# Reading the first block's keys once: tap shifts on TensorE in a fused gated long-convolution and SwiGLU kernel

## The chip, the core and the metric

The kernel runs on one core of one Trainium2 chip. A core has TensorE (matrix multiply, PE in the profile; PEld is its weight load), VectorE (DVE), ScalarE (ACT), GpSimd (POOL) and SyncE (SP), which here only issues transfers; 16 DMA engines move data between HBM and SBUF, the on-chip memory of 128 partitions. Matmul results land in PSUM. The metric is the device time of one execution in microseconds (us), lower is better.

## The reference

Two sub-layers run over a sequence of 2048 tokens with 640 channels, all tensors bf16:

```
ln(x)    = (x - mean(x)) / sqrt(var(x) + 1e-5)               # over the 640 channels
kshift   = sum over t = 0..3 of  k[s - t] * shift_k[:, t]    # a causal filter of four taps; rows before 0 are zero
kv       = kshift * v
y        = causal_conv(kv, ssm_k) + kv * ssm_D               # 2048 taps per channel (by FFT in the reference)
h        = q + ln(q) * y
out      = h + (silu(ln(h) @ w_gate) * (ln(h) @ w_up)) @ w_down       # 640 -> 1728 -> 640
```

## The kernel before, in words

**Tiling.** The sequence is cut into four blocks of 512 tokens (`n` = 0..3), a block into four tiles of 128 tokens (`q` = 0..3), one token per partition. The long convolution becomes a sum of block products in a transformed domain of 2 x 512 coefficients ("c" and "s" halves, four row tiles of 128 each). The filter's four blocks are transformed once (`g_transform(p)`: 64 matmuls against the basis `WG`, evicted by ACT, L296). Block n's `kv` is transformed by `x_transform(n)` (32 matmuls against `WX`, evicted by ACT, L364). `pair(j, p)` multiplies block j's transform with the filter's part p elementwise on DVE (eight operations of 128x2560 for a whole pair). `inverse(n)` goes back to tokens by matmuls against `WI`, adds the mirrored half by matmuls against a reversal matrix `flip`, multiplies with `ln(q)`, adds q, computes the second layer norm, and hands the result to `ffn(n)` by a transposing DMA into `hT`. `ffn(n)` makes 14 column chunks: five gate matmuls into bank 0 of a PSUM tile, five up matmuls into bank 1, silu (L530) and a copy (L531) on ACT, a product on DVE (L533), and then 112 down matmuls (L542).

**The taps.** `front(n)` makes `kv`. For each tile, `front_tile` holds four shifted copies of k side by side (`k4`, 128 x 4 x 640, read by one overlapping DMA of 640 KB a tile), multiplies them with the tap weights `w4` (L315), adds them in two steps (L316, L317) and multiplies with v (L318). In block 0, `first_loads` fetches the four shifted tiles by k loads of 560, 640 and 1280 KB and four small ones from POOL for the rows at the edge, which a POOL memset (L332) zeroes first. `w4` is spread over the partitions by `wcast`: a matmul with a row of ones and an ACT copy for each tap (L278, L280). The first two tiles of `kv` are also reversed in token order by matmuls with `flip` (L347) into `rev`, and L350 and L351 form the difference and the sum that `x_transform` takes.

**Layer norms.** `ln` takes the sums by two ACT passes (L436: mean, L437: mean square; the order between them is free), except for the second layer norm of block 0, which DVE does. POOL then runs four tiny operations (L443 to L446) to get 1/sqrt(var + eps), and DVE scales (L451).

**Order of work.** Every operation is given to a planner with an engine, an assumed duration, what it reads and writes, a priority `pr` (lower first) and sometimes an earliest time `t0`. `Plan.order` runs a list schedule over these, and the instructions are written out in that order, so each engine's queue is fixed in advance. PSUM has two tiles each of kind A (front, x_transform, inverse) and F (g_transform, ffn). Assumed durations are helpers: `act(n)` for an eviction, a lag of 0.12 us from one engine to another, 1.7 us for the POOL part of a layer norm. Transfers go through the queues of SP and ACT, and a few through POOL; the planner models eight transfers in flight, and a ninth waits for the oldest. Two instructions that touch the same PSUM tile are ordered in the order they are written, even where they touch different banks of it. In block 0 the filter's part 0 has priority -5, ahead of the front (0 to 3) and of `x_transform(0)` (8).

## Time and profile before

| | us |
|---|---|
| median of 5 runs (310.83 to 312.32) | 311.78 |
| the profiled execution's own time | 311.13 |
| its span, first to last instruction | 309.3 |
| PE busy | 269.1 (87%), 1540 matmuls recorded |
| DVE busy | 231.1 (75%), 307 instructions |
| ACT busy | 164.6 (53%) |
| POOL busy | 112.3 (36%) |
| moved by DMA | 45.94 MB |

Busy time of an engine is the union of its instructions' spans; matmuls are pipelined, so PE can be busy without running at its peak. The table of stages gives busy time by stretch of the span; the timeline lists instructions with start, duration, and in brackets the idle time of the engine before them with what released it; the chain is the sequence of work that ended last, followed back from the end. A row's line number is that of the code above.

### The profile page before, as it was taken

The page shows a single profiled execution, that of the slowest core. Times are in us where ns is not written, and L with a number is a line of the kernel's source. Part 1 is how long each engine was busy: PE and PEld are TensorE (multiplying, and loading weights), DVE is VectorE, ACT ScalarE, POOL GpSimd, SP SyncE. Part 2 cuts the span into 40 slices and gives each one's busy share as a digit, 9 for nine tenths or more (in the row PEclk, how much of TensorE's full clock was granted, in tenths as well). Part 3 has the DMA queues.
Part 4 walks back from the last instruction along what each step waited for, and adds up shares of the span by engine and source line. Part 5 has one row for each costly group of instructions (what it writes and reads, how often), then busy time and mean ns, then how long its engine had stood idle before and what let it go on. Part 6 is the DMA issues. An engine that isn't in the chain of part 4 may idle for free.

```text
span 309.3 us, 4282 instructions
## 1 busy us (share of the span) xinstructions
PE 269.1 (87%) x1540; PEld 151.1 (49%) x1556; DVE 231.1 (75%) x307; ACT 164.6 (53%) x318; POOL 112.3 (36%) x132
## 2 busy tenths in 40 slices
...
GB/s 186 316 352 188 375 184 208 2 126 329 214 85 127 99 172 215 135 291 176 87 123 68 105 210 190 103 201 85 138 147 57 24 95 32 130 143 133 0 45 42
DMA packets 71943, 45.94 MB, mean 149 GB/s; under 512 B 30772, under 2 KB 69492, under 8 KB 71794
## 3 DMA queue, kind: packets, MB, share of 16 engines
...
q8 instruction: 12, 0.20, 0.3%
q0 software_dynamic: 160, 0.08, 0.1%
q14 instruction: 9, 0.07, 0.1%
...
## 4 chain that ended last, share of the span: by engine, by line
PE 39%; DVE 32%; DMA 13%; ACT 6%; issue 5%; POOL 4%; ACTq 0%; POOLq 0%; DVEq 0%
PE psF L524 22%; DVE s L369 10%; PE psF L542 8%; DMA s<-const_wg 5%; PE psF L293 4%; DVE T L369 4%; DMA hT<-hl 4%; PE psA L361 4%; DVE k L315 3%; DMA WI<-const_wi 2%; DVE tT L533 2%; DVE y L490 2%; DVE o L547 2%; POOL sm L443 2%; ACT uc L531 1%
## 5 line engine op out<-in xcount | busy, mean ns | idle before, releaser
L443 POOL TENSOR_TENSOR sm<-sm 128x1 f32<-128x1 f32 x28 | 40.5, 1445 | 117.1 <-ACT junk L436 117.1
L524 PE MATMUL psF<-hT,wg 128*128 128x512 bf16 x268 | 69.9, 384 | 9.6 <-DMA hT<-hl 8.7
L524 PE MATMUL psF<-hT,wu 128*128 128x512 bf16 x256 | 65.3, 384 | 2.9 <-ACT sg L530 2.2
L542 PE MATMUL psF<-wd,tT 128*128 128x320 bf16 x448 | 64.9, 299 | 1.1 <-ACT uc L531 0.9
L530 ACT ACTIVATE sg<-psF 128x512 bf16<-128x512 f32 (+1 forms) x56 | 33.5, 598 | 53.6 <-PE psF L524 53.6
L542 PEld LDWEIGHTS <-tT 128*128 128x128 bf16 x448 | 41.4, 97 | 24.7 <-issue 9.6
L524 PEld LDWEIGHTS <-wg 128*128 128x128 bf16 x280 | 27.4, 99 | 41.8 <-issue 12.3
L533 DVE TENSOR_TENSOR tT<-sg,uc 128x512 bf16<-128x512 bf16 (+1 forms) x56 | 23.6, 422 | 32.4 <-ACT uc L531 32.2
L369 DVE TENSOR_TENSOR s<-s,T 128x2560 bf16<-128x2560 bf16 x32 | 47.3, 1486 | 0.0
L369 DVE TENSOR_TENSOR T<-s,s 128x2560 bf16<-128x2560 bf16 x32 | 47.3, 1486 | 0.0
L524 PEld LDWEIGHTS <-wu 128*128 128x128 bf16 x260 | 25.6, 99 | 33.2 <-issue 5.4
L293 PE MATMUL psF<-wd,s 128*128 128x320 bf16 x192 | 29.8, 314 | 9.9 <-DMA s<-const_wg 9.5
L293 PEld LDWEIGHTS <-s 128*128 128x128 bf16 x256 | 25.8, 101 | 21.8 <-DMA s<-const_wg 10.2
L531 ACT CAST uc<-psF 128x512 bf16<-128x512 f32 (+1 forms) x56 | 32.6, 582 | 5.6 <-PE psF L524 5.5
L446 POOL TENSOR_TENSOR sm<-sm,mhalf 128x1 f32<-128x1 f32 x32 | 31.6, 989 | 2.7
L296 ACT CAST s<-psF 128x640 bf16<-128x640 f32 x32 | 22.1, 694 | 17.3 <-PE psF L293 17.3
L361 PE MATMUL psA<-kv,WX 128*128 128x320 bf16 x128 | 22.1, 316 | 4.7 <-DMA WI<-const_wi 3.9
L436 ACT ACTIVATE junk<-x 128x640 bf16<-128x640 bf16 x28 | 20.7, 740 | 3.6 <-DVE x L491 3.3
L547 DVE TENSOR_TENSOR o<-psF,x 128x640 bf16<-128x640 f32 x16 | 13.1, 819 | 12.5 <-PE psF L542 12.5
L364 ACT CAST s<-psA 128x640 bf16<-128x640 f32 x32 | 21.4, 702 | 0.7 <-PE psA L361 0.5
L437 ACT ACTIVATE junk<-x 128x640 bf16<-128x640 bf16 x28 | 20.8, 743 | 0.4
L315 DVE TENSOR_TENSOR k<-k,w 128x2560 bf16<-128x2560 bf16 x14 | 20.7, 1484 | 0.3 <-DMA k<-in_A_k_dram 0.3
...
## 6 DMA issues: line engine op xcount, KB each, us to landing
...
```

Source lines behind the costliest of these rows:

```text
L293: nc.tensor.matmul(ps(g)[:, h, 0:NH], WG[:, kt, ct * P:(ct + 1) * P], gT[p][:, kt, h * NH:(h + 1) * NH], start=(kt == 0), stop=(kt == 3))
L296: add("ACT", act(D), lambda g=g, ct=ct: nc.scalar.copy(r3(G[p][ct // 4][:, ct % 4, :]), ps(g)[:, :, 0:NH]), r=[g], w=[Gk[p] + "cs"[ct // 4 ...
L315: add("DVE", dve(4 * D), lambda: nc.vector.tensor_mul(kd[:], kd[:], w4[:]), r=["w4"] + ks, w=[kn], pr=pr)
L361: nc.tensor.matmul(ps(g)[:, h, 0:NH], WX[:, kt, ct * P:(ct + 1) * P], kv[:, base + kt, h * NH:(h + 1) * NH], start=(kt == 0), stop=(kt == 1))
L369: add("DVE", dve(n * D), lambda: f(o, a, b), r=ks(ak) + ks(bk), w=ks(ok), after=["WG0", "WG1"] if ok[:2] == "s7" else [], pr=pr)
L443: e.tensor_tensor(s[:, 2:3], s[:, 0:1], s[:, 0:1], op=ALU.mult)
L446: e.tensor_tensor(s[:, 4:5], s[:, 3:4], mhalf[:], op=ALU.pow)
L524: nc.tensor.matmul(ps(gr)[:, which, :], w[:, kt, cc * P:(cc + 1) * P], hT[b][:, kt, :], start=(kt == 0), stop=(kt == 4))
L530: add("ACT", act(MB), lambda gr=gr, s=s, z=z: nc.scalar.activation(sg[s][:z, :], ps(gr)[:z, 0, :], ACT.Silu), r=[(gr, 0)], w=[f"sg{s}"], p ...
L531: add("ACT", act(MB), lambda gr=gr, s=s, z=z, merged=merged: nc.scalar.copy(uc[s][:z, :], ps(gr)[64:128, 0, :] if merged else ps(gr)[:, 1, ...
L533: add("DVE", dve(MB), lambda c=c, s=s, z=z: TM(tT[:z, c * MB:(c + 1) * MB], sg[s][:z, :], uc[s][:z, :]), r=[f"sg{s}", f"uc{s}"], w=[f"tT{c ...
L542: nc.tensor.matmul(ps(gr)[:, h, 0:NH], tT[:z, c * MB + m * P:c * MB + (m + 1) * P], wd[:z, c, h * NH:(h + 1) * NH], start=(c == 0), stop=( ...
```

## The change

k of block 0 is loaded once (640 KB, `kfirst`, into the buffer of block 1's x). `front_first` multiplies each k tile with all four taps in one DVE operation (the k tile is repeated by a broadcast operand), and the shift by 0 to 3 rows together with the sum over taps is done on PE: eight matmuls for the first tile, fourteen for each of the others (three taps also take rows from the tile before), with 128-column windows of a constant `perm` that holds an identity, its mirror image and zeros. For the first two tiles the window is mirrored, so the result comes out reversed; v of these two tiles is reversed on PE too and copied out by ACT. DVE multiplies the PSUM result with v. Three of the eight evictions of `x_transform(0)` go to DVE. `g_transform(0)` has priority 9 instead of -5, and the evictions of every `g_transform` go ahead of ACT's other work.

In the layer norm, ACT's first pass gives minus the mean and the second pass takes it as its bias, so that it sums squared deviations; POOL does two operations instead of four. In the feed-forward part, silu (bank 0) and the up matmuls (bank 1) are declared independent of each other. The planner's lag from one engine to another becomes 0.22 us from PE and 0.24 us from ACT, `act(n)` becomes shorter, and some priorities and earliest times are set anew. Nothing else of the computation changes.

```diff
...
 def make_flip():
-    f = np.eye(P)[::-1]
-    return np.ascontiguousarray(np.stack([f, -f], axis=1)).astype(ml_dtypes.bfloat16)
+    i, z = np.eye(P), np.zeros((P, P))
+    j = i[::-1]
+    return np.ascontiguousarray(np.stack([-j, z, j, z, i, z], axis=1)).astype(ml_dtypes.bfloat16)
...
             for u in users[i]:
-                lag = 0.0 if ops[u]["eng"] == e and e != "DVE" and not o["kb"] else 0.12
+                lag = LAG.get(e, 0.12) if ops[u]["eng"] != e or o["kb"] else 0.12 if e == "DVE" else 0.0
...
 RATE = 330.0
+LAG = {"PE": 0.22, "ACT": 0.24}
...
 def act(n):
-    return 0.19 + n / 1200
+    return 0.07 + n / 1220
...
     slot = [tl(f"s{i}", [P, 8, D]) for i in range(8)]
-    last, fourth = slot[7], slot[4]
+    last = slot[7]
...
     WI = tl("WI", [P, 8, 256])
-    flip = tl("flip", [P, 2, P])
+    perm = tl("perm", [P, 6, P])
+    flip = (perm[:, 2, :], perm[:, 0, :])
+    band = perm[:].rearrange("p a b -> p (a b)")[:, 3 * P:6 * P]
+    mirrored = perm[:].rearrange("p a b -> p (a b)")[:, P:4 * P]
...
     xin = [tl(f"x{i}", [P, 4, D]) for i in range(2)]
+    kfirst = xin[1]
+    products, prodk = [k4[0], k4[1], slot[4][0], slot[4][1]], ["k4_0", "k4_1", "s4c", "s4s"]
...
     hl = [tl(f"hl{i}", [P, D]) for i in range(2)]
-    drow = y[0][0:1, :]
+    drow = xln[0][0:1, :]
...
-    add("POOL", 0.1, lambda: nc.gpsimd.memset(ones[:], 1.0), w=["ones"], pr=-9)
+    add("POOL", 0.1, lambda: nc.gpsimd.memset(ones[:], 1.0), w=["ones"], pr=-99)
...
     add("ACT", 1.5, lambda: nc.scalar.activation(sg[0][0:1, 0:P], ones[:], ACT.Silu), r=["ones"], w=["sg0"], pr=-50)
-    load("POOL", drow, A_ssm_D.partition_broadcast(1), ["drow"], -75, 5)
+    load("ACT", drow, A_ssm_D.partition_broadcast(1), ["drow"], -95.5, 5)
...
             add("ACT", act(D), lambda g=g, ct=ct: nc.scalar.copy(r3(G[p][ct // 4][:, ct % 4, :]), ps(g)[:, :, 0:NH]),
-                r=[g], w=[Gk[p] + "cs"[ct // 4]], pr=pr, rel=("F", g))
+                r=[g], w=[Gk[p] + "cs"[ct // 4]], pr=pr - 900, rel=("F", g))
...
         kd, kn, vb, vn = k4[b], f"k4_{b}", vt[b], f"v{b}"
-        if n == 0:
-            vb, vn = hT[0][:].rearrange("p a b -> p (a b)")[:, q * D:(q + 1) * D], "v0all"
-            if q > 1:
-                kd, kn = slot[4][b], "s4" + "cs"[b]
-        else:
-            load("SP", kd[:], run(r0 - 3, P), [kn], pr - 40, 640)
-            load("SP", vb[:], vv[r0:r0 + P, :], [vn], pr - 40, 160)
-        ks = [kn] + [f"edge{i}" for i in range(5) if n == 0 and q == 0]
+        load("SP", kd[:], run(r0 - 3, P), [kn], pr - 40, 640)
+        load("SP", vb[:], vv[r0:r0 + P, :], [vn], pr - 40, 160)
+        ks = [kn]
...
     def first_loads():
-        kd = k4[0]
-        load("ACT", kd[16:128, :, :], run(13, 112), ["edge4"], -98, 560)
-        load("SP", k4[1][:], run(P - 3, P), ["k4_1"], -88, 640)
-        load("ACT", hT[0][:].rearrange("p a b -> p (a b)").rearrange("p (a b) -> p a b", a=4), vv[0:MB, :].rearrange("(m p) d -> p m d", p=P), ["v0all"], -97, 640)
-        load("ACT", WG, WG_h.ap(), ["WG0", "WG1"], -96, 1024)
-        load("SP", fourth[:].rearrange("p (m a) b -> p m (a b)", m=2),
-             bass.AP(tensor=kk.tensor, offset=kk.offset + (2 * P - 3) * D, ap=[[D, P], [P * D, 2], [1, 4 * D]]), ["s4c", "s4s"], -87, 1280)
-        add("POOL", 2.2, lambda: nc.gpsimd.memset(kd[0:32, :, :], 0.0), w=["k4_0"], pr=-90)
-        for t in range(3):
-            k = 3 - t
-            load("POOL", kd[t:t + 1, k:4, :], kk[0:t + 1, :].rearrange("(o a) d -> o a d", o=1), [f"edge{t}"], -80, 2, r=["k4_0"])
-        load("POOL", kd[3:16, :, :], run(0, 13), ["edge3"], -81, 65, r=["k4_0"])
+        load("SP", kfirst[:], kk[0:MB, :].rearrange("(m p) d -> p m d", p=P), ["x1_0", "x1_1", "x1_2", "x1_3"], -98, 640)
+        load("ACT", hT[0][:].rearrange("p a b -> p (a b)").rearrange("p (a b) -> p a b", a=4), vv[0:MB, :].rearrange("(m p) d -> p m d", p=P), ["v0all"], -96, 640)
+        load("ACT", WG, WG_h.ap(), ["WG0", "WG1"], -95, 1024)
+    def front_first(q, pr):
+        prod, pk = products[q][:], prodk[q]
+        add("DVE", dve(4 * D), lambda: nc.vector.tensor_mul(prod, kfirst[:, q:q + 1, :].to_broadcast([P, 4, D]), w4[:]), r=["w4", f"x1_{q}"], w=[pk], pr=pr)
+        g = ("A", "S", q)
+        m, turn = 1 - q, q < 2
+        def mm():
+            for h in range(2):
+                cols = slice(h * NH, (h + 1) * NH)
+                for i, (src, t, last_tile) in enumerate([(products[q], t, 0) for t in range(4)] + [(products[q - 1], t, 1) for t in range(3) if q]):
+                    j = 3 - t
+                    lhs = mirrored[:, P * (1 - last_tile) + j:][:, 0:P] if turn else band[:, P * (1 + last_tile) - j:][:, 0:P]
+                    nc.tensor.matmul(ps(g)[:, h, 0:NH], lhs, src[:, t, cols], start=(i == 0), stop=(i == (6 if q else 3)))
+        add("PE", (14 if q else 8) * 0.137, mm, r=["flip", pk] + ([prodk[q - 1]] if q else []), w=[g], pr=pr - 50, acq=("A", g))
+        v = hT[0][:].rearrange("p a b -> p (a b)")[:, q * D:(q + 1) * D]
+        if turn:
+            gv = ("F", "V", q)
+            def mv():
+                for h in range(2):
+                    nc.tensor.matmul(ps(gv)[:, h, 0:NH], flip[0], v[:, h * NH:(h + 1) * NH], start=True, stop=True)
+            add("PE", 2 * 0.137, mv, r=["flip", "v0all"], w=[gv], pr=pr - 60, acq=("F", gv))
+            add("ACT", act(D), lambda: nc.scalar.copy(r3(y[q][:]), ps(gv)[:, :, 0:NH]), r=[gv], w=[f"y{q}"], pr=pr - 60, rel=("F", gv))
+            add("DVE", dve(D, True), lambda: nc.vector.tensor_mul(r3(rev[:, m, :]), ps(g)[:, :, 0:NH], r3(y[q][:])), r=[g, f"y{q}"], w=["rev"], pr=pr, rel=("A", g))
+        else:
+            add("DVE", dve(D, True), lambda: nc.vector.tensor_mul(r3(kv[:, q, :]), ps(g)[:, :, 0:NH], r3(v)), r=[g, "v0all"], w=[f"kv{q}"], pr=pr, rel=("A", g))
...
         for q in (0, 1, 2, 3):
-            front_tile(n, q, pr + q)
-            if q < 2:
+            (front_tile(n, q, pr + q) if n else front_first(q, pr + q))
+            if q < 2 and n:
...
                     for h in range(2):
-                        nc.tensor.matmul(ps(g)[:, h, 0:NH], flip[:, 0, :], kv[:, q, h * NH:(h + 1) * NH], start=True, stop=True)
+                        nc.tensor.matmul(ps(g)[:, h, 0:NH], flip[0], kv[:, q, h * NH:(h + 1) * NH], start=True, stop=True)
...
             add("PE", 4 * 0.137, mm, r=["WX", f"kv{base}", f"kv{base + 1}"], w=[g], pr=pr, acq=("A", g), after=[Xk[n] + "cs"[ct // 4]])
-            add("ACT", act(D), lambda g=g, ct=ct: nc.scalar.copy(r3(X[n][ct // 4][:, ct % 4, :]), ps(g)[:, :, 0:NH]),
+            on_dve = n == 0 and ct in (1, 7, 4)
+            copy = nc.vector.tensor_copy if on_dve else nc.scalar.copy
+            add("DVE" if on_dve else "ACT", dve(D, True) if on_dve else act(D), lambda g=g, ct=ct, copy=copy: copy(r3(X[n][ct // 4][:, ct % 4, :]), ps(g)[:, :, 0:NH]),
...
-    def ln(n, q, which, pr, vec=False):
+    def ln(n, q, which, pr, vec=False, t0=0.0):
...
         else:
-            add("ACT", act(D) + 0.2, lambda: nc.scalar.activation(junk[:], src, ACT.Copy, scale=1.0 / D, accum_out=s[:, 0:1]), r=[xk], w=[k + "a"], pr=pr)
-            add("ACT", act(D) + 0.2, lambda: nc.scalar.activation(junk[:], src, ACT.Square, scale=float(D ** -0.5), accum_out=s[:, 1:2]), r=[xk], w=[k + "b"], pr=pr)
+            add("ACT", act(D) + 0.25, lambda: nc.scalar.activation(junk[:], src, ACT.Copy, scale=-1.0 / D, accum_out=s[:, 0:1]), r=[xk], w=[k + "a"], pr=pr, t0=t0)
+            add("ACT", act(D) + 0.45, lambda: nc.scalar.activation(junk[:], src, ACT.Square, bias=s[:, 0:1], accum_out=s[:, 1:2]), r=[xk, k + "a"], w=[k + "b"], pr=pr)
...
         def fin():
-            if vec:
-                e.tensor_scalar(s[:, 3:4], s[:, 1:2], 1.0, EPS, op0=ALU.mult, op1=ALU.add)
-            else:
-                e.tensor_tensor(s[:, 2:3], s[:, 0:1], s[:, 0:1], op=ALU.mult)
-                e.tensor_tensor(s[:, 3:4], s[:, 1:2], s[:, 2:3], op=ALU.subtract)
-                e.tensor_scalar(s[:, 3:4], s[:, 3:4], 1.0, EPS, op0=ALU.mult, op1=ALU.add)
+            e.tensor_scalar(s[:, 3:4], s[:, 1:2], 1.0 if vec else 1.0 / D, EPS, op0=ALU.mult, op1=ALU.add)
             e.tensor_tensor(s[:, 4:5], s[:, 3:4], mhalf[:], op=ALU.pow)
-        add("POOL", 1.0 if vec else 1.7, fin, r=[k + "a", k + "b"], w=[k], pr=pr)
+        add("POOL", 1.5, fin, r=[k + "a", k + "b"], w=[k], pr=pr)
...
         s = sm[n, q, which]
-        nc.vector.tensor_scalar(dst, xin[n % 2][:, q, :], s[:, 0:1], s[:, 4:5], op0=ALU.subtract, op1=ALU.mult)
+        nc.vector.tensor_scalar(dst, xin[n % 2][:, q, :], s[:, 0:1], s[:, 4:5],
+                                op0=ALU.subtract if (n, which) == (0, 2) else ALU.add, op1=ALU.mult)
...
     def load_x(n, pr, queue="SP"):
-        load(queue, xin[n % 2][:], xq[n * MB:(n + 1) * MB, :].rearrange("(m p) d -> p m d", p=P), [f"x{n % 2}_{q}" for q in range(4)], pr, 640, t0=(10, 30, 0, 0)[n])
+        load(queue, xin[n % 2][:], xq[n * MB:(n + 1) * MB, :].rearrange("(m p) d -> p m d", p=P), [f"x{n % 2}_{q}" for q in range(4)], pr, 640, t0=(14, 30, 0, 0)[n])
         for q in range(4):
-            ln(n, q, 1, pr + 30)
+            ln(n, q, 1, pr + 30, t0=(26, 50, 0, 0)[n])
...
                             for part in range(2):
-                                nc.tensor.matmul(ps(g)[:, h, 0:NH], flip[:, part, :], (es, os_)[part][m][:, h * NH:(h + 1) * NH],
+                                nc.tensor.matmul(ps(g)[:, h, 0:NH], flip[part], (es, os_)[part][m][:, h * NH:(h + 1) * NH],
...
     wcount = [0]
+    issued = {}
+    def apart(gr, bank, inst):
+        for other in issued.get((gr, 1 - bank), []):
+            tc.declare_no_dep(inst.ins if hasattr(inst, "ins") else inst, other, reason="other bank")
+        issued.setdefault((gr, bank), []).append(inst.ins if hasattr(inst, "ins") else inst)
...
                     for kt in range(5):
-                        nc.tensor.matmul(ps(gr)[:, which, :], w[:, kt, cc * P:(cc + 1) * P], hT[b][:, kt, :], start=(kt == 0), stop=(kt == 4))
+                        i = nc.tensor.matmul(ps(gr)[:, which, :], w[:, kt, cc * P:(cc + 1) * P], hT[b][:, kt, :], start=(kt == 0), stop=(kt == 4))
+                        if which:
+                            apart(gr, 1, i)
+                def silu(gr, s, z):
+                    apart(gr, 0, nc.scalar.activation(sg[s][:z, :], ps(gr)[:z, 0, :], ACT.Silu))
...
                 z = 64 if merged else P
-                add("ACT", act(MB), lambda gr=gr, s=s, z=z: nc.scalar.activation(sg[s][:z, :], ps(gr)[:z, 0, :], ACT.Silu), r=[(gr, 0)], w=[f"sg{s}"], pr=pr - 9000)
+                add("ACT", act(MB), lambda gr=gr, s=s, z=z, silu=silu: silu(gr, s, z), r=[(gr, 0)], w=[f"sg{s}"], pr=pr - 9000)
...
-    load("ACT", flip[:], J_h.ap(), ["flip"], -26, 64, t0=6)
+    load("ACT", perm[:], J_h.ap(), ["flip"], -97, 192)
...
     load("ACT", WX[:], WX_h.ap(), ["WX"], -25, 512, t0=8)
-    g_transform(0, -5)
+    g_transform(0, 9)
...
     gload(2, -20)

```

## The prediction, made before the changed kernel was run

> **What bounds the kernel now.** I read the table of stages first. The columns are the stretch in us, its length, busy time of each engine with instruction counts, granted clock, DMA share and GB/s.
>
> ```profile
> 0.00:45.30 45.30, 24.50 (x138) 14.91 (x139) 20.66 (x29) 23.11 (x42) 13.99 (x28) 0.96 1.00 272
> 45.30:76.40 31.10, 28.52 (x206) 19.89 (x204) 30.96 (x48) 23.90 (x44) 16.85 (x24) 1.00 0.53 155
> 76.40:257.70 181.30, 168.50 (x954) 92.22 (x968) 170.24 (x214) 102.45 (x205) 81.45 (x80) 1.00 0.51 138
> 257.70:309.30 51.60, 47.58 (x244) 24.04 (x247) 9.25 (x18) 15.13 (x28) 0.00 (x0) 0.95 0.28 74
> ```
>
> DVE works 20.66 of the first 45.30 us. From the first pair product (45.32) to the last feed-forward part (257.7) it works 201.2 of 212.4, so this stretch is DVE's. The last 51.6 us are PE's (`ffn(3)`), and cannot start before DVE has finished `inverse(3)`. So the time is: idle time of DVE up to 45.3, plus DVE's work, plus a PE tail. Next the chain of waits for the start, to see what keeps DVE idle.
>
> ```profile
> 3.90 15.47 DMA s<-const_wg
> 19.42 11.05 PE psF L293 x64
> 30.77 6.28 DMA WI<-const_wi
> 37.06 3.99 PE psA L361 x16
> ```
>
> The filter basis lands at 19.4, part 0 of the filter fills PE until 30.5, and the first `x_transform` comes only at 37.0. It does not read WI; the timeline shows what really came last:
>
> ```profile
> 13.52 2.87 DVE L315 TENSOR_TENSOR k<-k,w 128x2560 bf16<-128x2560 bf16 x2
> 19.40 2.88 DVE L315 TENSOR_TENSOR s<-s,w 128x2560 bf16<-128x2560 bf16 x2
> 32.74 0.43 PE L347 MATMUL psA<-kv,flip 128*128 128x320 bf16 x2
> 33.21 0.69 ACT L349 CAST rev<-psA 128x640 bf16<-128x640 f32 x1 [0.70 <-PE psA L347]
> 33.94 0.83 DVE L350 TENSOR_TENSOR kv<-kv,rev 128x1280 bf16<-128x1280 bf16 x1 [8.58 <-ACT rev L349]
> 36.08 0.82 DVE L351 TENSOR_TENSOR kv<-kv,rev 128x1280 bf16<-128x1280 bf16 x1
> 45.32 1.48 DVE L369 TENSOR_TENSOR s<-s,s 128x2560 bf16<-128x2560 bf16 x1
> ```
>
> DVE had the tile products of block 0 at 25.4; the two reversals stood in PE's queue behind the filter, DVE idled 8.58 us, and L351 (ends 36.90) released `x_transform`. Last, the waits from 45 to 257:
>
> ```profile
> DVE hl L451 <- POOL sm L446: 4.4, 5, 1.3
> DVE tT L533 <- ACT uc L531: 1.9, 4, 1.0
> PE psF L524 <- ACT sg L530: 2.2, 4, 0.9
> ```
>
> The layer norm's POOL part costs DVE 4.4 us in five waits, and PE waits 2.2 us for silu of the other bank.
>
> **Part 1, the tap weights and k.** Before, DVE starts at 13.52 because `w4` is complete at 12.84. From its first matmul (6.20, held by a POOL memset) that takes 6.6 us, of which 2.45 are ACT standing behind the WX load (issued 11.18). The memset of ones now comes first on POOL, and five loads instead of four are issued by ACT ahead of the table load (1.28): at 0.4 to 0.5 each that is 3.1 + 1.28 + 0.3 = 4.7 for the first eviction's earliest start. When the 5 KB weight row lands is not shown: by 6.2 at the latest, not before its issue ends at 1.3. I take 4, and 4 + 4.2 = 8.2 (7 to 11). k is first on SP's queue; the nearest rows are 640 KB in 8.7 us and 560 KB in 8.2, while 5.58 MB moved in the first 20 us. Now about 3.8 MB are asked for (k, v, perm, WG, two filter parts), so 7 us, landed at 7.7 (5 to 9.4). Products start at 8.2 instead of 13.5.
>
> **Part 2, DVE work of block 0.** Removed: L316 four times (3.08) and L317 four times (1.75). L318 (0.44 each, 1.75) becomes a product from PSUM at 0.82 (row L490), 3.28. Three evictions are added at the same 0.82, 2.46. The 480 ns add, four products (5.92 at 1.48) and L350/L351 (1.65) stay: 13.8 instead of 14.5, 0.7 less. The broadcast product is in no row: it is at best 1.48, at worst at the one-element rate of L490, 2560/640 x 0.74 = 2.96, which is 5.9 more in all. I take 1.48, since element step and type are those of L315.
>
> **Part 3, PE.** Added 50 shift matmuls and 4 for v, removed 4 reversals. A warm 320-column matmul comes every 0.137 us (eight in 1.09, between evictions at 25.06 and 26.15). After idle they take twice that: the first two filter groups were evicted at 21.77 and 23.90, 2.1 apart. So 16 x 0.27 + 38 x 0.137 = 9.5 us, beginning when the first product ends, 8.2 + 1.5 = 9.7: it would end at 19.2, about when DVE, at 9.2 us for four products and four PSUM products, reaches the fourth tile. One or two filter groups (1.1 each) put between them delay the last tile; with L350/L351 I take 23 for `kv` (21 to 26), 14 us before 36.9. WG has perm and v ahead on ACT's queue (832 KB, before: 1200 KB and more beside it); I take 15 (12 to 19.4). Filter 8.8 and `x_transform` 4.4 bring PE's total from 9.7 to 22.7, plus 1 to 2 of idling: 34. The first pair product needs only the "c" halves, so DVE starts it at 33 (30 to 37), against 45.32.
>
> ACT's evictions (eight and five at 0.69, two for v) make 10.4 us between 10 and 34, beside PE. The three on DVE fall where it has only block 1 to do.
>
> **Part 4, what DVE had done by then.** Before, it had also done 6.2 us of block 1 (20.66 - 14.46). Those loads go out on SP from 29.88, after the filter transposes. SP's queue loses 1280 KB; at some 160 KB/us (half of 320 GB/s, two queues) that is 8 us: issued from 22, landed from 27 (4.8 median). kfirst and the first transpose still precede gT1, and perm is 128 KB more on ACT. Between 27 and 33, less the evictions, DVE does 4.5 (2 to 6.2). Gain on DVE: 45.32 - 33 - (6.2 - 4.5) = **10.6** (6 to 15).
>
> **Part 5, the first feed-forward part on PE.** Its start at 76.44 waited for `hT`, landed 76.35. PE must by then have done 54 + 32 + 256 + 32 + 8 matmuls and two reversals, 384 x 0.137 = 52.6, 2.2 for the cold ones, from 9.7, with some 3 idle: 67.5, while DVE offers 65.8. PE gains 8.9, DVE 10.6. PE has slack later (168.5 busy of 181.3, and these ends are modelled), so I take 9.6 of the two.
>
> **Part 6, silu.** Its 2.2 us of PE waits go. Silu also starts one bank earlier (0.5 us of the 0.60 and 0.58 pair leaves the path to L533). PE does not bind there, so I count 0.8 (0 to 2.2).
>
> **Part 7, layer norm.** 56 POOL operations go; L443 (1445 ns) ran beside ACT's second pass, only L444 (525 ns) behind it. The second pass now has to wait for the first's accumulator and reads a bias. No row has either; ACT's own order bounds the wait below at 0, and the 0.17 to 0.47 that ACT stood idle before filter evictions (L296), which wait on PE, bound it above: at 0.3, 28 x 0.3 = 8.4 us of ACT at 53% busy. On DVE's waits (4.4 in five) it may gain 2 or lose 5 x 0.3 = 1.5; I take 0. The Trainium skill, "ScalarE: Activation LUTs", section "What ACT_TABLE_LOAD costs", speaks against this part: an operand of one value per partition adds about 93 ns to an ACTIVATE; by that an estimate of 2.6 us for 28 passes, and no run here shows it. The same skill, "VectorE: DVE Perf Modes", section "The DRAIN you can't avoid", says that an accumulator read by the engine's next instruction is read stale without a semaphore; the trace has no such pair.
>
> **Part 8, the planner.** For an eviction of 512 columns its duration and lag were 0.617 + 0.12 and are 0.49 + 0.24: the sum is the same. Order changes everywhere; in this stretch DVE's idle time is 11.2 us of 212, so up to 4 either way, taken as 0.
>
> **Sum.** The profiled execution took 311.13, 0.65 under the median; 311.13 - 9.6 - 0.8 = 300.7, and against the median 301.4.
>
> **Rivals.** (a) Partial gain: the pair starts earlier, but the front is dearer or FFN 0 waits for PE. For it: the broadcast bound (5.9 us more on DVE), cold matmuls, PE at 28.5 of 31.1 us before FFN 0. Against it: the step is the same as L315's. With 4 to 6 us less gain: 305 to 307. Chance 0.20. (b) Slower: the new order puts L533 ahead of its copy on ACT while DVE is the bound. There are 42 such products before 257.7; they waited 1.9 us in all. If each waits 0.3 the loss is 12.6 and the time 314; it decides from 0.25 each (10.4/42). For it: every operation is reordered, and ACT's second pass becomes longer than its assumed 0.45 more. Against it: copies come earlier with silu, and duration plus lag add up as before. Chance 0.11. (c) More gain: pair at 30, all of block 1's 6.2 us done, both silu and POOL waits gone: 311.8 - 15 - 4 = 293. Chance 0.08. (d) No effect, because FFN 0 is held by its weights or by hT: the trace has weights issued from 32.2, well ahead. Chance 0.03.
>
> **Numbers.** Likeliest 301.4, chance 0.58, own range 297 to 305. With (a) and part of (c) the range is 295 to 309. A change of 0.3% (0.9 us) is about what a measurement can tell: faster 0.86, same 0.03, slower 0.11.
>
> **What would show it.** Right: first product near 8 us, at 1.48; L351's successor ends near 23; first pair product near 33; FFN 0's first matmul at 66 to 68, FFN 3's near 248, and the tail still 51.6. No PE wait for silu. Wrong: a broadcast product over 2 us; the last shift group behind several filter groups; DVE waits on L533 summing to over 5 us before FFN 3; FFN 0 waiting for PE.

## The result and the profile after

| us | before | after | predicted |
|---|---|---|---|
| median (85 and 43 runs) | 311.17 | 312.84 | 301.4 |
| the profiled execution's own time | 311.13 | 312.32 | |
| its span | 309.3 | 310.5 | |
| first pair product on DVE | 45.32 | 41.60 | 33 |
| first matmul of FFN 0 on PE | 76.44 | 78.01 | 66 to 68 |
| first matmul of FFN 3 on PE | 257.70 | 259.92 | 248 |
| from there to the end of the span | 51.60 | 50.58 | 51.6 |

The ratio to before is 0.999, with a 95% interval of 0.9971 to 1.0009: no difference. The changed kernel's single times scatter from 307 to 319 us, those of before from 308.6 to 316.3; the ratio leaves disturbed executions out and the medians do not, which is why these two differ.

The stages of the changed kernel's profile, with the columns of the prediction's first lines, cut at its own first pair product and at FFN 3:

```profile
0.00:41.60 41.60, 25.93 (x150) 16.03 (x151) 16.77 (x17) 13.37 (x22) 0.42 (x6) 1.00 1.11 241
41.60:259.92 218.32, 202.67 (x1198) 116.64 (x1210) 203.61 (x268) 136.15 (x267) 114.73 (x64) 0.98 0.52 139
259.92:310.50 50.58, 46.62 (x244) 23.87 (x247) 9.24 (x18) 16.56 (x28) 0.00 (x0) 0.97 0.28 75
```

The pair starts 3.7 us earlier. From it to FFN 3 the time grew from 212.4 to 218.3: DVE has 203.6 us of work there instead of 201.2, because less of block 1 was done by then, and idles 14.7 instead of 11.2. So FFN 3 starts 2.2 us later, and the end gains 1.0. The start decides the rest. Its DMA issues and PE and DVE work in the timeline of after:

```profile
1.23 23.23 SPq L276 DMA_TRANSPOSE wd<-in_A_ssm_k_dram  x3
7.44 2.89 DVE L335 TENSOR_TENSOR k<-x,w 128x2560 bf16<-128x2560 bf16 x2 [7.44 <-ACT w L288]
16.56 1.22 PE L353 MATMUL psF<-hT,perm 128*128 128x320 bf16 x4 [5.29 <-DMA hT<-in_A_v_dram]
19.48 0.48 DVE L292 TENSOR_TENSOR wd<-wd,xln 1x640 bf16<-1x640 bf16 x1 [9.15 <-DMA wd<-in_A_ssm_k_dram]
28.10 0.82 DVE L373 TENSOR_TENSOR kv<-kv,rev 128x1280 bf16<-128x1280 bf16 x1
37.33 1.49 DVE L318 TENSOR_TENSOR k<-k,w 128x2560 bf16<-128x2560 bf16 x1 [3.35 <-DMA k<-in_A_k_dram]
39.61 0.70 PE L383 MATMUL psA<-kv,WX 128*128 128x320 bf16 x4 [2.94 <-DVE s L388]
41.60 1.49 DVE L393 TENSOR_TENSOR s<-s,s 128x2560 bf16<-128x2560 bf16 x1
```

The tap products begin at 7.44 and take 1.45 each, with the broadcast operand. Then two things are late at once. v, issued at 1.67, lands at 16.56 and PE idles 5.29 for it. And DVE's queue has the one-row addition of `ssm_D` (L292) ahead of the third product; it waits until 19.48 for part 0 of the filter, DVE idles 9.15, and the last two products and all that follows them stand behind it. (The two waits overlap: from 16.56 on v was there.) `kv` is complete at 28.9. The groups of issues (KB, us to landing):

```profile
s<-const_wg ACTq DMA_DIRECT2D x1, 1024.0 KB, 16.7
hT<-in_A_v_dram ACTq DMA_DIRECT2D x1, 640.0 KB, 14.9
wd<-in_A_ssm_k_dram SPq DMA_TRANSPOSE x3, 18.4
```

Three transposing loads of the filter now go out on SP right behind k. The table of stretches of 6 us shows what the 16 DMA engines did at that time (the last two columns; the share adds up the packets' times and can pass 1):

```profile
6.00:12.00 6.00, 2.96 (x11) 1.30 (x10) 2.89 (x2) 1.29 (x2) 0.00 (x0) 1.00 1.12 277
12.00:18.00 6.00, 1.44 (x6) 0.84 (x6) 0.00 (x0) 0.71 (x2) 0.00 (x0) 1.00 1.50 75
18.00:24.00 6.00, 5.21 (x28) 3.09 (x26) 4.52 (x5) 0.57 (x1) 0.00 (x0) 1.00 1.12 203
```

Between 12 and 18 the engines are busy throughout and move 75 GB/s. Before, the 1.9 MB of k loads stood between the first and the second filter transpose in SP's queue, and these stretches moved 307, 336 and 320 GB/s; the middle one was:

```profile
12.00:18.00 6.00, 0.00 (x0) 0.00 (x0) 4.89 (x6) 0.83 (x2) 0.00 (x0) 1.00 1.07 336
```

The second half of the loss stands at FFN 0, rows of SP's queue and of PE in after:

```profile
71.34 2.99 SPq L515 DMA_TRANSPOSE hT<-hl  x1
69.80 6.85 PE L301 MATMUL psF<-hT,s 128*128 128x320 bf16 x48 [0.17 <-ACT s L304]
78.01 1.24 PE L551 MATMUL psF<-hT,wg 128*128 128x512 bf16 x4 [1.36 <-DMA hT<-hl]
```

PE transforms filter parts until 76.6. Before, it had 32 matmuls of part 1 done by the first pair product; here it had none, and 8 of part 0 were left: 40 x 0.137 = 5.5 us, about as much as the stretch from the pair to FFN 0 grew (36.4 instead of 31.1). That this work is the cause is argued from the count. PE's last wait at FFN 0 is another: 1.36 us for `hT`. DVE had written its last `hl` at 69.7 (before: 71.4), but the transposing load of it was issued at 71.34, behind another one and a load of `w_down`. Before, PE waited 1.49 us for `hT` at the same place.

The waits after the start, up to FFN 3 (us, times, longest): PE's wait for silu is gone, DVE's waits for POOL sum to 4.4 as before, and PE's for `hT` to 6.7 against 8.7, both with the one at FFN 3. New is one wait of DVE for an eviction:

```profile
DVE y L499 <- ACT os L492: 4.1, 1, 4.1
DVE xln L470 <- POOL sm L465: 3.0, 2, 2.5
DVE hl L470 <- POOL sm L465: 1.4, 2, 0.7
PE psF L551 <- DMA hT<-hl: 6.7, 2, 5.3
```

### The profile page after: what moved, and what is told of

Same layout as the page of the kernel before. It is cut to its first block, busy times and chain, and to the rows that moved or that the text cites. A ratio compares the mean times of both kernels' runs of the same rounds, so it can differ in the third digit from the quotient of the medians.

```text
span 310.5 us, 4308 instructions
## 1 busy us (share of the span) xinstructions
PE 275.2 (89%) x1591; PEld 156.5 (50%) x1606; DVE 229.6 (74%) x302; ACT 166.1 (53%) x315; POOL 115.2 (37%) x70
## 3 DMA queue, kind: packets, MB, share of 16 engines
HBM read 35.97 MB, written 2.62 MB: 124 GB/s over the span
## 5 line engine op out<-in xcount | busy, mean ns | idle before, releaser
L464 POOL TENSOR_SCALAR sm<-sm 128x1 f32<-128x1 f32 x32 | 57.3, 1792 | 137.2 <-ACT junk L461 130.0
L465 POOL TENSOR_TENSOR sm<-sm,mhalf 128x1 f32<-128x1 f32 x32 | 57.4, 1793 | 2.7
L565 DVE TENSOR_TENSOR tT<-sg,uc 128x512 bf16<-128x512 bf16 (+1 forms) x56 | 23.6, 422 | 30.2 <-ACT uc L563 30.2
L563 ACT CAST uc<-psF 128x512 bf16<-128x512 f32 (+1 forms) x56 | 32.8, 585 | 16.6 <-PE psF L551 16.1
L301 PEld LDWEIGHTS <-s 128*128 128x128 bf16 x256 | 25.0, 98 | 11.1 <-issue 1.1
L301 PE MATMUL psF<-wd,s 128*128 128x320 bf16 x192 | 27.9, 299 | 0.3 <-ACT s L304 0.3
L488 PE MATMUL psA<-s,WI 128*128 128x320 bf16 x128 | 20.1, 314 | 4.3 <-DVE s L393 4.3
L460 ACT ACTIVATE junk<-x 128x640 bf16<-128x640 bf16 x28 | 20.8, 742 | 5.5 <-DVE x L511 4.7
L461 ACT ACTIVATE junk<-x,sm 128x640 bf16<-128x640 bf16 x28 | 23.4, 836 | 0.2
L383 PE MATMUL psA<-kv,WX 128*128 128x320 bf16 x128 | 20.2, 299 | 3.5 <-DVE s L388 2.9
L388 ACT CAST s<-psA 128x640 bf16<-128x640 f32 x29 | 19.0, 710 | 3.7 <-PE psA L383 3.7
## 6 DMA issues: line engine op xcount, KB each, us to landing
s<-const_wg ACTq DMA_DIRECT2D x1, 1024.0 KB, 16.7
```

Source lines behind the costliest of these rows:

```text
L301: nc.tensor.matmul(ps(g)[:, h, 0:NH], WG[:, kt, ct * P:(ct + 1) * P], gT[p][:, kt, h * NH:(h + 1) * NH], start=(kt == 0), stop=(kt == 3))
L460: add("ACT", act(D) + 0.25, lambda: nc.scalar.activation(junk[:], src, ACT.Copy, scale=-1.0 / D, accum_out=s[:, 0:1]), r=[xk], w=[k + "a"] ...
L461: add("ACT", act(D) + 0.45, lambda: nc.scalar.activation(junk[:], src, ACT.Square, bias=s[:, 0:1], accum_out=s[:, 1:2]), r=[xk, k + "a"], ...
L464: e.tensor_scalar(s[:, 3:4], s[:, 1:2], 1.0 if vec else 1.0 / D, EPS, op0=ALU.mult, op1=ALU.add)
L465: e.tensor_tensor(s[:, 4:5], s[:, 3:4], mhalf[:], op=ALU.pow)
L488: nc.tensor.matmul(ps(g)[:, h, 0:NH], WI[:, 4 * part + ct, m * P:(m + 1) * P], a[part][:, ct, h * NH:(h + 1) * NH], start=(ct == 0), stop= ...
```

## The experiments

### One part of the change alone

The first has the start alone: the changed kernel with layer norm, silu and planner as before.

```diff
-            add("ACT", act(D) + 0.25, lambda: nc.scalar.activation(junk[:], src, ACT.Copy, scale=-1.0 / D, accum_out=s[:, 0:1]), r=[xk], w=[k + "a"], pr=pr, t0=t0)
-            add("ACT", act(D) + 0.45, lambda: nc.scalar.activation(junk[:], src, ACT.Square, bias=s[:, 0:1], accum_out=s[:, 1:2]), r=[xk, k + "a"], w=[k + "b"], pr=pr)
+            add("ACT", act(D) + 0.2, lambda: nc.scalar.activation(junk[:], src, ACT.Copy, scale=1.0 / D, accum_out=s[:, 0:1]), r=[xk], w=[k + "a"], pr=pr, t0=t0)
+            add("ACT", act(D) + 0.2, lambda: nc.scalar.activation(junk[:], src, ACT.Square, scale=float(D ** -0.5), accum_out=s[:, 1:2]), r=[xk], w=[k + "b"], pr=pr)
...
-                        if which:
-                            apart(gr, 1, i)
...
-    return 0.07 + n / 1220
+    return 0.19 + n / 1200
```

> The kernel before with the first-block part alone (k read once, shifts on TensorE, three evictions on VectorE, the filter transform behind the front); layer norm, silu and the planner's constants as before. Theory A (the front itself starts the first pair only some 4 us earlier, because three filter transposes now queue together beside v and the basis, and PE is no earlier at the first feed-forward part): first pair near 41 to 42 us, first feed-forward matmul at 75 to 79, time within 1.5 us of before. Rival B (the front gains, another part gives it back): 4 to 8 us faster than before.

The second has the layer norm alone, in the kernel before.

```diff
+            add("ACT", act(D) + 0.45, lambda: nc.scalar.activation(junk[:], src, ACT.Square, bias=s[:, 0:1], accum_out=s[:, 1:2]), r=[xk, k + "a"], w=[k + "b"], pr=pr)
```

> The kernel before with the new layer norm alone (second ScalarE pass reads the first's mean, two GpSimd operations). Theory A: within 1.5 us of before either way. Rival B (GpSimd operations starved between VectorE operations give back the front's gain): 3 to 6 us slower.

The third has silu alone, in the kernel before.

```diff
+                        if which:
+                            apart(gr, 1, i)
...
+                    apart(gr, 0, nc.scalar.activation(sg[s][:z, :], ps(gr)[:z, 0, :], ACT.Silu))
```

> The kernel before with silu and the up matmuls declared independent, nothing else. Prediction's term: 0.8 us faster (0 to 2.2). Theory A and rival B both allow that. Silu should start about 1.1 us earlier than its up matmuls end, and no PE wait for silu should be left.

The fourth has the planner's constants alone, in the kernel before.

```diff
+LAG = {"PE": 0.22, "ACT": 0.24}
...
-    return 0.19 + n / 1200
+    return 0.07 + n / 1220
```

> The kernel before with the planner's new lags and eviction durations alone, so that only the order of instructions changes. Theory A: within 1.5 us of before. Rival C (the new order costs what the front gains): 3 to 6 us slower.

Measured, with the kernel before at 314.9 us in the same session (19 runs, 310.2 to 318.8): the start alone 315.23 (ratio 1.0086, 1.0007 to 1.0165), the layer norm alone 317.36 (four runs, 311.3 to 318.75, too far apart for a ratio), silu alone 320.82 (1.0252, 1.0109 to 1.0395, from three runs), the planner alone 310.92 (0.994, 0.9887 to 0.9992). The planner's term lies inside its bounds, the layer norm's can't be told, and the other two are missed: the predicted 9.6 us of the start are not there at all, though its first pair product is at 40.98, and its FFN 0 comes at 83.35, later than the 75 to 79 expected. Silu alone is slower, and neither the prediction nor the expectation had that. The profiled execution (322.99 us, the longest of the four) shows two things beside silu's own: the first pair product comes at 50.65 instead of 45.32, and DVE's waits for POOL sum to 12.1 us over the whole span, against 5.1 before:

```profile
DVE xln L451 <- POOL sm L446: 7.1, 2, 4.0
DVE hl L451 <- POOL sm L446: 5.0, 6, 1.3
```

Why its start is late was not followed up.

So two questions were open: what holds the start, and why POOL's few short operations cost more as soon as the order changes.

### The filter transposes out of the way of v and WG

First, parts 1 to 3 wait for WG, through a copy of one element by POOL into their destination.

```diff
     def gload(p, pr):
+        if p in (1, 2, 3):
+            add("POOL", 0.2, lambda: nc.gpsimd.tensor_copy(gT[p][0:1, 0, 0:1], WG[0:1, 0, 0:1]), r=["WG0"], w=[f"gT{p}"], pr=pr)
         add("SP", 2.7, lambda: nc.sync.dma_start_transpose(gT[p], A_ssm_k[:, p * MB:(p + 1) * MB]), w=[f"gT{p}"], pr=pr, kb=640)
```

> The changed kernel, with the filter transposes of parts 1 to 3 held until the basis WG has landed (a one-element GpSimd copy from WG into each destination, so that the transfer must wait for it). Theory A (the slow transposes share the DMA engines with v and WG and delay both): v lands near 7 instead of 16.5, WG near 12 instead of 19.3, the first pair starts near 33 to 36 instead of 41.6, and the time falls by 3 to 7 us. Rival D (the DMA engines are full of other work anyway): v and WG land within 2 us of where they did, time within 1.5 us.

Second, the one-row addition moves from DVE to POOL.

```diff
-    add("DVE", 0.2, lambda: nc.vector.tensor_add(gT[0][0:1, 0, :], gT[0][0:1, 0, :], drow), r=["drow"], w=["gT0"], pr=-20)
+    add("POOL", 1.0, lambda: nc.gpsimd.tensor_add(gT[0][0:1, 0, :], gT[0][0:1, 0, :], drow), r=["drow"], w=["gT0"], pr=-20)
```

> The changed kernel, with the one-row addition of ssm_D to the first filter part on GpSimd instead of VectorE, so that VectorE's products no longer stand behind it. Theory A: VectorE's third and fourth product move from 19.9 and 22.0 to near 11 to 14, but TensorE still stands behind v (16.5), so the first pair starts only 1 to 3 us earlier, time 0 to 2 us less. Rival E (the wait in VectorE's queue is what costs): first pair 6 to 9 us earlier, time 4 to 8 us less.

Third, both of these.

```diff
+        if p in (1, 2, 3):
...
+    add("POOL", 1.0, lambda: nc.gpsimd.tensor_add(gT[0][0:1, 0, :], gT[0][0:1, 0, :], drow), r=["drow"], w=["gT0"], pr=-20)
```

> Both edits: transposes held, addition on GpSimd. Theory A: first pair at 31 to 34, the start as it had been predicted; if the start sets the end, the time falls by 6 to 9 us against the changed kernel; if PE's filter transforms or later waits set it, by less than 3, and the first feed-forward matmul stays after 74.

Fourth, both, and all of block 0's `x_transform` evictions on ACT.

```diff
-            on_dve = n == 0 and ct in (1, 7, 4)
+            on_dve = False
```

> As the kernel with both edits, and the three evictions of the first transform back on ScalarE. Theory A: PE's 2.9 us of waiting for an eviction that stands on VectorE behind a k transfer goes; first pair earlier by 0 to 3 us than with both edits alone.

Measured against before at 310.86 us (309.88 to 311.92, seven runs):

| | median us | ratio (95%) | v's landing after issue | first pair product | FFN 0 |
|---|---|---|---|---|---|
| transposes 1 to 3 held | 301.82 | 0.9669 (0.9607 to 0.9731) | 10.1 | 38.12 | 74.9 |
| addition on POOL | 308.33 | 0.9888 (0.9837 to 0.9939) | 17.6 | 45.03 | 82 |
| both | 299.91 | 0.9527 (0.9445 to 0.961) | 10.7 | 31.59 | 68.56 |
| both, evictions on ACT | 299.12 | 0.9625 (0.9585 to 0.9665) | 10.0 | 33.19 | 70.0 |

Each trace column is from one profiled execution; that with the addition on POOL took 312.34, the longest of its four, and its v was the latest of these four kernels. So its pair at 45.03 says little about the addition, and its median shows a gain of 1%. With both edits the start comes near where it was predicted (pair 33, FFN 0 at 66 to 68), and the time with it. Holding is most of the effect, more than the 3 to 7 us expected; the addition's place seems to matter too, since without it the pair is at 38.12 with nearly the same landing of v. The evictions make no difference that can be told.

But holding also puts block 1's first k and v ahead of the transposes. So the next kernel keeps the changed kernel's order and its bytes, and takes away only the transposing: parts 1 to 3 are plain loads of as many bytes. (Their contents are not the filter's; this kernel leaves the transposition of these parts out.)

```diff
     def gload(p, pr):
+        if p:
+            add("SP", 2.7, lambda: nc.sync.dma_start(out=gT[p], in_=vv[p * MB:(p + 1) * MB, :].rearrange("(m p) d -> p m d", p=P)), w=[f"gT{p}"], pr=pr, kb=640)
+            return
         add("SP", 2.7, lambda: nc.sync.dma_start_transpose(gT[p], A_ssm_k[:, p * MB:(p + 1) * MB]), w=[f"gT{p}"], pr=pr, kb=640)
```

> The changed kernel in its order, with the transfers of filter parts 1 to 3 made plain ones of the same bytes (640 KB each, rows of v instead of the transposed filter; so these parts of the filter are not the reference's). Theory A (transposing transfers move some 70 GB/s while they hold the DMA engines, and v and WG share the engines with them): v lands near 7 to 9, WG near 13 to 15, VectorE's products go on near 12, first pair at 32 to 36, time 5 to 10 us under the changed kernel. Rival F (the bytes ahead of v and WG count, not that they are transposed, or block 1's k loads behind them in SP's queue): v and WG land within 3 us of 16.5 and 19.3, first pair after 39.

It took 304.43 us against 311.85 (0.9753, 0.9639 to 0.9868). Its issues and its stretches, columns as above:

```profile
s<-const_wg ACTq DMA_DIRECT2D x1, 1024.0 KB, 11.4
hT<-in_A_v_dram ACTq DMA_DIRECT2D x1, 640.0 KB, 9.7
...
12.00:18.00 6.00, 3.00 (x21) 1.96 (x20) 3.17 (x4) 1.29 (x2) 0.00 (x0) 1.00 1.07 360
```

With the same bytes in the same order, the stretch from 12 to 18 moves 360 GB/s instead of 75, v lands in 9.7 instead of 14.9, WG in 11.4 instead of 16.7, the pair starts at 33.52. So it is the transposing that makes the start late, not the amount asked for. (The plain loads also read rows of another tensor; what in a transposing load costs the time was not separated.)

### Undoing the other parts, with one transpose still in flight

In the kernel with both edits, silu's order of before.

```diff
-                        if which:
-                            apart(gr, 1, i)
```

> The kernel with transposes held and the addition on GpSimd, with silu and the up matmuls ordered again as before the change. Prediction's term: 0.8 us slower than with the independent silu (0 to 2.2). Rival G (independent silu costs, as the single look at it alone hinted): 1 to 5 us faster.

The same with the layer norm of before.

```diff
-            add("ACT", act(D) + 0.45, lambda: nc.scalar.activation(junk[:], src, ACT.Square, bias=s[:, 0:1], accum_out=s[:, 1:2]), r=[xk, k + "a"], w=[k + "b"], pr=pr)
+            add("ACT", act(D) + 0.2, lambda: nc.scalar.activation(junk[:], src, ACT.Square, scale=float(D ** -0.5), accum_out=s[:, 1:2]), r=[xk], w=[k + "b"], pr=pr)
```

> The kernel with transposes held and the addition on GpSimd, with the layer norm's passes as before (free order on ScalarE, four GpSimd operations). Prediction's term: 0 (faster by up to 2 or slower by 1.5 for the new form). Rival B (two long GpSimd operations are starved and delay VectorE): faster by 2 to 5.

The same with the planner's constants of before.

```diff
-    return 0.07 + n / 1220
+    return 0.19 + n / 1200
```

> The kernel with transposes held and the addition on GpSimd, with the planner's lags and eviction durations as before the change. Prediction's term: 0, up to 4 either way; as a part alone the new constants made 0.6% less, so 1 to 3 us slower is expected here.

Silu undone: 299.64 (293.77 to 302.9), not to be told from 299.91. Layer norm undone: 311.17 (306.04 to 315.85; 0.9837, 0.9752 to 0.9922). Planner undone: 295.87, 296.27, 297.37 and, the profiled one, 313.05. That last execution was inconclusive for the planner and told something else. Its one transpose, its v, and its stretches:

```profile
1.24 11.48 SPq L278 DMA_TRANSPOSE wd<-in_A_ssm_k_dram  x1
...
hT<-in_A_v_dram ACTq DMA_DIRECT2D x1, 640.0 KB, 22.6
...
6.00:12.00 6.00, 0.70 (x3) 0.18 (x2) 4.29 (x3) 1.29 (x2) 0.00 (x0) 1.00 1.19 86
18.00:24.00 6.00, 0.00 (x0) 0.00 (x0) 0.00 (x0) 0.00 (x0) 0.00 (x0) 1.00 1.21 119
```

One transposing load beside v and WG was in flight here, and v took 22.6 us. In the profiled executions with this one transpose in flight, v took 6.9, 10.0, 10.1, 10.7, 18.4 and 22.6. A comparison of parts is worth little while that is open.

### No transpose in flight until WG has landed

Now part 0 waits for WG as well, and its issue stands behind the first loads.

```diff
-        if p in (1, 2, 3):
+        if p in (0, 1, 2, 3):
...
     first_loads()
+    gload(0, -90)
+    add("POOL", 1.0, lambda: nc.gpsimd.tensor_add(gT[0][0:1, 0, :], gT[0][0:1, 0, :], drow), r=["drow"], w=["gT0"], pr=-20)
```

> The changed kernel with all four filter transposes, part 0 included, waiting for WG through a one-element POOL copy, and the ssm_D add on POOL. Theory A (the transposing transfers beside v and WG make the start late, and one of them is enough for it in some executions): v lands 6 to 8 us after its issue, WG by about 12, part 0 of the filter some 6 to 8 us behind WG (18 to 21), first pair product 31 to 35, first matmul of FFN 0 at 67 to 72, time 294 to 301, and the single times lie within 4 us of each other. Rival B (the scatter has another origin, for instance the transfers of k, v and WG among themselves): v still takes 15 us or more in some executions and the single times spread over 8 us or more, as those of the kernels with one transpose in flight. Rival C (now the filter is the late one): PE waits for part 0, first pair product past 38, time 303 to 308.

And in this kernel, the layer norm, silu and the planner of before, one at a time, with the three edits of the last section.

```diff
-            add("ACT", act(D) + 0.45, lambda: nc.scalar.activation(junk[:], src, ACT.Square, bias=s[:, 0:1], accum_out=s[:, 1:2]), r=[xk, k + "a"], w=[k + "b"], pr=pr)
+            add("ACT", act(D) + 0.2, lambda: nc.scalar.activation(junk[:], src, ACT.Square, scale=float(D ** -0.5), accum_out=s[:, 1:2]), r=[xk], w=[k + "b"], pr=pr)
```

> hold0 with the layer norm of before (two independent ScalarE passes, three more POOL operations each). Theory A (the layer norm's change is worth about nothing, as predicted; what the earlier run without it lost came from a late start): within 2 us of hold0. Rival B (the POOL operations stand in DVE's way): 4 to 12 us slower than hold0 with the same first pair product, and DVE's waits for POOL's sm sum to 8 us or more instead of about 4.

```diff
-                        if which:
-                            apart(gr, 1, i)
```

> hold0 with silu's order of before (silu behind the whole bank). Theory A (0.8 us predicted, 0 to 2.2): 0 to 2.5 us slower than hold0, PE's wait for sg returns at about 2 us before FFN 3. Rival B (silu's wait costs DVE too): 3 us or more slower. Rival C: no difference or faster by up to 1 us.

```diff
-    return 0.07 + n / 1220
+    return 0.19 + n / 1200
```

> hold0 with the planner's durations and lags of before, so that only the order of the work changes. Theory A (0, up to 4 either way): within 2 us of hold0. Rival B (the new constants cost): 3 to 4 us faster than hold0, with less idle time of DVE between the first pair product and FFN 3.

Measured against before at 311.69 us (17 runs):

| | median us (lowest to highest) | ratio (95%) | v's landing | pair | FFN 3 |
|---|---|---|---|---|---|
| all four held | 303.43 (303.06 to 304.89) | 0.9756 (0.9713 to 0.9799) | 6.6 | 32.36 | 252.00 |
| layer norm of before | 314.27 (311.66 to 316.94) | 1.0076 (1.0044 to 1.0109) | 6.5 | 31.51 | 259.31 |
| silu of before | 305.59 (304.78 to 306.77) | 0.9825 (0.9784 to 0.9866) | 6.5 | 33.05 | 253.01 |
| planner of before | 305.92 (302.85 to 308.9) | 0.979 (0.9727 to 0.9852) | 6.6 | 30.96 | 252.19 |

v lands in 6.5 to 6.6 in all four, and the single times of the first lie within 1.8 us, those of the third within 2.0; with the layer norm or the planner of before 5 to 6 us remain. So the transpose beside v was behind most of the scatter of the kernels with one in flight, and not all of it. The time of the first is above the 294 to 301 expected, and its FFN 0, at 72.88, is later than the 67 to 72: v and WG are early now, but DVE waits 3.48 us before the first pair product for the evictions of the filter's part 0, which has become late. For the changed kernel's own scatter, with three in flight, it is the likely cause, not a shown one.

The layer norm is worth 10.8 us between the medians here, where nothing was predicted. The stages of the held kernel, then of the one with the old layer norm, from the first pair product to FFN 3:

```profile
32.36:252.00 219.64, 205.14 (x1213) 118.12 (x1225) 207.61 (x270) 137.14 (x268) 69.56 (x64) 0.99 0.56 148
```

```profile
31.51:259.31 227.80, 208.01 (x1214) 119.46 (x1225) 207.29 (x270) 132.79 (x260) 107.31 (x118) 0.97 0.53 142
...
DVE xln L475 <- POOL sm L470: 7.9, 3, 4.0
DVE hl L475 <- POOL sm L470: 2.5, 3, 1.0
DVE hl L475 <- POOL sm L468: 1.2, 1, 1.2
```

DVE's work is the same (207.6 and 207.3), its idle time 12.0 and 20.5. Its waits for POOL sum to 11.6 with the old layer norm and to 3.5 with the new one, which is nearly all of that. (These two executions differ by 7.3 us, which the 8.5 us of idle time cover; the medians differ by 10.8. PE was granted 0.97 of its clock with the old layer norm in this stretch and 0.99 with the new one, and over whole executions mostly 0.967 against 0.986 to 0.989; what that adds to the 7.3 was not separated.) The timeline of the one with the old layer norm shows how such a wait comes about (lines of this kernel: L467 to L470 are POOL's four operations):

```profile
140.29 13.52 POOL L467 TENSOR_TENSOR sm<-sm 128x1 f32<-128x1 f32 x1 [19.26 <-ACT junk L460]
...
152.28 1.48 DVE L393 TENSOR_TENSOR s<-s,T 128x2560 bf16<-128x2560 bf16 x1
153.89 0.19 POOL L468 TENSOR_TENSOR sm<-sm 128x1 f32<-128x1 f32 x1
154.17 0.19 POOL L469 TENSOR_SCALAR sm<-sm 128x1 f32<-128x1 f32 x1
154.45 0.55 POOL L470 TENSOR_TENSOR sm<-sm,mhalf 128x1 f32<-128x1 f32 x1
...
156.38 0.45 DVE L475 TENSOR_SCALAR xln<-x,sm 128x640 bf16<-128x640 bf16 x1 [2.62 <-POOL sm L470]
```

A POOL operation on one column starts at 140.29 and is done at 153.81, when DVE's run of two-input products has ended (153.76). Then POOL's operations take 0.19 and 0.55 again, and DVE stands for 2.62 until two tiles' statistics are through. The old layer norm has four such operations for a tile and the new one two, so the chain that DVE waits for is half as long. The Trainium skill, "SBUF — State Buffer", section "Who interferes with whom", names a reason: a DVE instruction with two inputs in SBUF takes the second through the read port that a GpSimd instruction needs for reading SBUF, and this shared port is an exclusive lock. The rows agree with it, and go further: POOL was kept out not for one DVE instruction but for a run of them. No run here takes DVE's products away, so the port itself is argued, and the coincidence of the times is what is shown.

Silu is worth 2.2 us between the medians; PE's wait for it comes back in the kernel without it:

```profile
PE psF L551 <- ACT sg L557: 2.4, 3, 1.0
```

The planner's constants can't be told from nothing here: the intervals overlap.

### Part 0 behind v alone

WG had landed by about 11, and part 0's issue was at 11.77 in the held kernel. Here it waits for v alone.

```diff
-            add("POOL", 0.2, lambda: nc.gpsimd.tensor_copy(gT[p][0:1, 0, 0:1], WG[0:1, 0, 0:1]), r=["WG0"], w=[f"gT{p}"], pr=pr)
+            add("POOL", 0.2, lambda: nc.gpsimd.tensor_copy(gT[p][0:1, 0, 0:1], (WG[0:1, 0, 0:1] if p else hT[0][0:1, 0, 0:1])), r=["WG0" if p else "v0all"], w=[f"gT{p}"], pr=pr)
```

> hold0, but part 0's transpose waits for v alone (landed at about 8.2) and not for WG (landed at about 12.5); parts 1 to 3 still wait for WG. Theory A (a transposing transfer delays what is in flight beside it): v still lands in 6 to 7 us, WG lands later than in hold0, at 13 to 18, part 0 of the filter is there 2 to 4 us earlier than in hold0, first pair product at 29 to 33, time 299 to 304, single times within 4 us. Rival B (with v safe, WG is thrown back to 20 or later in some executions, and the scatter of 8 us returns, median over 304).

And the same with all evictions of block 0 on ACT.

```diff
-            on_dve = n == 0 and ct in (1, 7, 4)
+            on_dve = False
```

> hold0_v with all of block 0's x_transform evictions on ACT, as hold_add_evict. DVE loses 3 x 0.82 = 2.5 us, ACT gains 3 x 0.69 between 22 and 30. Theory A (DVE's work from the pair on is what counts): 1 to 3 us faster than hold0_v, 297 to 302. Rival B (PE is as full as DVE before the first feed-forward part, 205 us busy of 220): within 1 us of hold0_v.

Measured against before at 311.44 us (11 runs): 301.27 (299.78 to 302.19; 0.9652, 0.9596 to 0.9708), and 300.58 (298.74 to 301.0; 0.9625, 0.9574 to 0.9676). The timeline of the first of them:

```profile
8.95 13.10 SPq L278 DMA_TRANSPOSE wd<-in_A_ssm_k_dram  x3
12.09 3.47 PE L345 MATMUL psA<-k,perm 128*128 128x320 bf16 x14
19.20 3.42 PE L301 MATMUL psF<-wd,s 128*128 128x320 bf16 x24
30.50 1.49 DVE L393 TENSOR_TENSOR s<-s,s 128x2560 bf16<-128x2560 bf16 x1 [1.58 <-ACT s L388]
65.84 1.24 PE L551 MATMUL psF<-hT,wg 128*128 128x512 bf16 x5
250.63 1.24 PE L551 MATMUL psF<-hT,wg 128*128 128x512 bf16 x5 [1.37 <-DMA hT<-hl]
```

PE goes from the shifts to the filter without a gap, FFN 0 starts at 65.8. WG still lands 8.3 us after its issue: a transposing load that starts when WG has some 2 us left did it no harm, so the delay expected for WG did not come. The evictions' 2.5 us of DVE bring 0.7, within what these runs can tell. That is what rival B of the expectation had, by which PE is as full as DVE (205 us busy of 220 from the first pair product to FFN 3). Both kernels beat before and, by the ratio to it, the changed kernel, with single times within 2.5 us.

## Why the prediction was wrong

**The step that failed** is the transfers in part 1 and part 3. Part 1 counted 3.8 MB and priced them by the rate of the first 20 us of the trace of before. That rate is mostly that of plain loads; transposes, of which the first had stood ahead of 1.9 MB of k loads and the others behind, were counted by their bytes alone, and as two. In the changed kernel three of them are in flight at once beside v and WG, and 12 to 18 us moved 75 GB/s. k, issued ahead of them, was early (4.3 us after its issue, where 7 was counted), and the first product came at 7.44 against 8.2, when the tap weights were there. v had no term of its own: part 3 put it ahead of WG and let the shifts end at 19.2, and it landed at 16.56. WG's 15 came out at 19.3, inside the bounds given; `kv`'s 23 at 28.9, outside. The plain loads of the same bytes show it: 360 GB/s, pair at 33.52. PE's own term in part 3 holds: in the kernel with part 0 behind v alone the shifts end at 19.4 (19.2 predicted) and `kv` is complete at 21.9 (23).

**Part 2** kept "the 480 ns add" as a duration. Its size is right and its place is not: what stood behind it in DVE's queue was two products, and what it waited for was part 0's landing (9.15 us of idle DVE). The rest of part 2 holds, the broadcast product above all (1.45, taken as 1.48).

**Part 4.** Block 1's k was put at 22 to 27 by SP's bytes. The queue was held by the issue of transposes (1.23 to 24.46 for three, to 29.81 with the fourth), so it went out at 31.04 and landed at 37.3, and an eviction on DVE stood behind its product. The gain on DVE was 45.32 - 41.60 less 2.4 of work undone, that is 1.3, not 10.6.

**Part 5** took PE's work to set FFN 0, at "67.5" if the start is as predicted. In the ten kernels above whose pair started between 29.1 and 33.5 it was at 65.8 to 74.0. The lowest, with part 0 behind v alone, has PE at work up to FFN 0 without a wait there, as part 5 has it; the three highest, 72.9 to 74.0, are of the kernels whose part 0 stands behind WG. With the real start it was at 78.0, and the last wait was for `hT`.

**Part 6, silu,** was right in the changed order: the wait of PE is gone, and undoing it costs 2.2 us in the kernel with all transposes held, the upper end of 0 to 2.2 (with one transpose in flight, 299.64 against 299.91, it can't be told). Alone in the order of before it was slower, which the term did not have.

**Part 7, layer norm,** was mis-sized, and 0 stood for the wrong comparison. It was weighed against DVE's 4.4 us of waits for POOL in the order of before. With the old layer norm these waits are 3.3, 6.5, 11.6, 12.1 and 14.0 us in the five other orders tried, with the new one between 2.1 and 6.2 in fourteen. With all transposes held the new one is worth 10.8 us between the medians, 7.3 between the profiled executions, and without it the earlier start is worth nothing there: 314.27, and FFN 3 at 259.31, with the pair at 31.51. (With one transpose in flight two of four executions without it took 306.04 and 306.82, under before.) So it is luck that 301.27, the time with part 0 behind v alone, agrees with the predicted 301.4. The sum is another: FFN 0 comes 10.6 us earlier than before, FFN 3 only 7.1, and the stretch after it, counted as unchanged, takes 48.9 instead of 51.6; and the layer norm, counted as 0, keeps away waits that would have eaten the gain. Its price on ACT came out as the page that the prediction cited has it (the Trainium skill, "ScalarE: Activation LUTs", "What ACT_TABLE_LOAD costs", some 93 ns for an operand of one value per partition). The second pass before, then the first and the second pass in the changed kernel:

```profile
L437 ACT ACTIVATE junk<-x 128x640 bf16<-128x640 bf16 x28 | 20.8, 743 | 0.4
L460 ACT ACTIVATE junk<-x 128x640 bf16<-128x640 bf16 x28 | 20.8, 742 | 5.5 <-DVE x L511 4.7 <-DMA x<-in_A_q_dram 0.6
L461 ACT ACTIVATE junk<-x,sm 128x640 bf16<-128x640 bf16 x28 | 23.4, 836 | 0.2
```

836 less the 743 of before is 93 ns. The wait for the accumulator, bounded by 0.3, is 0.2 us for all 28.

**Part 8, the planner,** stays at 0 to what could be measured: 0.6% faster alone, not told apart in the held kernel.

**The rivals.** (a), partial gain, describes what happened at first: the pair starts earlier, and PE has work left before FFN 0; but it expected a gain of 4 to 6 us less, not none, and named the broadcast product and the cold matmuls as causes. (b) did not happen: up to FFN 3 DVE has no wait on ACT's copies for L565 (L533 before) in the changed kernel. (d), no effect, had the outcome, at a chance of 0.03. Of its two causes the weights did not hold FFN 0; `hT` did, for 1.36 us, but for 1.49 before as well, so it isn't what took the gain away. None of the four had the transposes, although the trace of before showed two things that speak of them: an issue of 22.52 us for two on SP (from 4.28), and 82 GB/s at a DMA share of 1.38 between 24 and 26 us.
